# Packed attention and routed experts: the first batch's scores in two column ranges, and four of its hidden blocks as split products

## The chip, the cores and the metric

One core of a Trainium2 chip. The metric is the device time of one execution, in microseconds (us); the time of a kernel is the median of its runs. Engines by their names in the profile: PE (matmuls) with PEld (its weight loads), DVE (VectorE), ACT (ScalarE), POOL (GpSimd), SP (SyncE, which here issues most DMAs).

## The reference, cut to what matters

```python
def sm_attn(qq, kk, vv):                       # scale = 1/8
    s = scale * qq @ kk.T;  s -= s.max(-1)
    a = exp(s);  a /= a.sum(-1) + 1e-9
    return a @ vv
p_packed = sm_attn(p, k, v)                    # 32 packed rows for each of 8 batches x 8 heads
x = sm_attn(q, p_packed, p_packed)             # 576 rows of 64 for each head -> (4608, 512)
logits = (x / |x|) @ (emb / |emb|).T / tau     # 8 experts
e = argmax(logits);  gate = softmax(logits)[e]
out = gate * (relu(x @ w1[e]) @ w2[e])         # 512 -> 1024 -> 512, fp32
```

## The kernel before

The eight batches are worked one after the other, each with its own 576 rows, eight heads in two groups of four (g = 0, 1; heads of a group lie side by side in 128 partitions). For each batch the kernel packs (32 packed rows for each head), guesses from the sum of the packed rows which expert the whole batch takes, loads that expert's w1 and w2 only, and later counts the rows that took another expert, which a loop at the end would redo. Every tile's engine is chosen by hand; each engine, and each DMA queue, runs its instructions in the order in which the program emits them.

Because a batch's x is its softmax times the packed rows, the first expert layer is done as softmax times G, where G is packed rows times w1 (128 rows for a group, 1024 columns in two halves fc = 0, 1). A product in full fp32 (two MATMUL records each) is used in a few places; most are "split": both factors are kept as a high and a low part (a cast, then a subtraction), and three products high x high, high x low, low x high are summed, each one MATMUL record (type fp32r).

The first batch goes ahead of the steady state, and the change is all in it:

- `begin` (lines 1024 to 1181) is emitted in pieces, each letter q of `PLAN` being one. Its first piece issues the loads of k, v and q (`load_whole`, `load_v`: lines 190, 201), turns the keys block by block on DVE (`flip`, lines 285 to 287), scores them on PE (`quarters`, line 238), takes maximum and exponential (350, 355), turns the result on PE (370), multiplies by v (390), sums the packed rows (402, 1096, 1101), and makes the guess (533 to 551; SP reads the index at line 551). `load_w1` (764) follows on SP, then k tiles of the second batch (175). After the guess come the transposes of q (1136) and its scores (1146). The fourth to sixth q pieces split the packed rows and their logits into `ppx` (274, 275), a factor of the routing products.
- `embeddings` (124) normalises the expert rows with a chain of small POOL steps (98 to 139), stepped by `next(emb_gen)`.
- The softmax of the first batch's 576 rows in two halves (hf = 0, 1) follows `ORDS`, one step for each letter s: U turn back, B biggest, S subtract, X exponential, T total, N normalise, R turn, H high part (619), L low part (623). `ENG` says for S, N and L, and for the four splits of G, whether POOL (p) or DVE (v) does them.
- `ffn` with late=True is the first batch's expert stage. It multiplies packed rows by w1 (853, `rows_w1`, g = 0 then 1), copies the result (863), and runs 16 hidden blocks: eight of half 0 (f0 to f7) and eight of half 1 (here h0 to h7). Before the change all of f0 to f7 are two full fp32 products each (872, one for each g; those of g = 0 of f0 to f3 early), and h0 to h7 are six split products each (893), which need all of G and of the high and low parts. Each block goes to one of four PSUM banks (tag pf), and the block four later waits until ACT's relu (897) and DVE's low part (898, and 903 in half 1) have read it. Then come eight steps over f at line 924 (the rest rows), interleaved with routing, and the output products (940).
- After each block the loop runs one string of `PLAN`: q a piece of `begin`, s a softmax step, G one split of G (`split_g`, 274 and 275), a a step of the second batch's attention (`att_main(1)`: scale and turn p, lines 301 and 302; four key flips; key scores, 260; maximum and exponential of each group, 350 and 355; turn of group 0, then of group 1 with its copies, 370 and 381 to 384; values, 390), w a split of w2 (`split_w2`, 785 on ACT and 786 on POOL), k a query flip (290, 294), r a step of routing (`route`, 680 on PE, 689 on DVE, 696 on ACT, five chunks through two PSUM tiles of tag pb).

## Time and profile before

| | us |
|---|---|
| runs of the kernel before | 444.05, 445.36, 445.59 (median 445.36) |
| the profiled execution: its own time | 444.3 |
| its span, first to last instruction | 442.6 |
| PE busy | 430.8 (97% of the span) |
| DVE, ACT, POOL busy | 303.3, 203.6, 150.2 |
| bytes moved by DMA | 88.22 MB, 199 GB/s in the mean |

The span is 1.7 us under the execution's own time, and the rows below are all of this one execution. A timeline row merges instructions of one line: start, time from the first start to the last end, engine, line, operation, tiles, shape, count, and in brackets the idle time before it with what ended it. PE's ends are modelled, so a stretch without an idle gap can still hold waits; the distance from one start to the next tells more.

### The profile page before, as it was taken

What the parts mean: (1) busy time and instruction counts of PE and PEld (TensorE: products, weight loads), DVE (VectorE), ACT (ScalarE), POOL (GpSimd) and SP (SyncE); (2) the same over time, 40 slices, a digit from 0 to 9 for tenths busy, and PEclk for the clock granted to TensorE, in tenths of its full rate; (3) what the DMA queues carried; (4) which work ended last, traced back from release to release, by engine and by line L of the source; (5) the groups of instructions that cost most, each with busy time, mean ns of one, the idle gap of its engine ahead of it and who ended that gap; (6) DMA issues with size and microseconds to landing.
All of it is one profiled execution on the core that took longest, in us unless ns stands there. A gap on an engine that the chain in (4) does not pass through costs nothing.

```text
span 442.6 us, 10441 instructions
## 1 busy us (share of the span) xinstructions
PE 430.8 (97%) x3762; PEld 339.4 (77%) x3763; DVE 303.3 (69%) x1006; ACT 203.6 (46%) x477; POOL 150.2 (34%) x201
## 2 busy tenths in 40 slices
PE   8799999999999999999999999999999999999994
PEld 6537768798787978879687977879687886879784
DVE  5568759669965899469883799558994698535400
ACT  2457632773237723465127723366235751466110
POOL 2538645342404441152504523044501534035000
PEclk9999999999999999999999999999999999999998
DMA  7999988877985479944995389843998206500011
GB/s 208 290 282 286 232 213 325 246 180 204 321 301 141 110 216 360 275 113 138 298 364 143 88 231 353 268 128 102 241 386 243 79 1 220 221 26 24 15 48 54
DMA packets 40267, 88.22 MB, mean 199 GB/s; under 512 B 10312, under 2 KB 19848, under 8 KB 40208
## 3 DMA queue, kind: packets, MB, share of 16 engines
q1 hardware_dynamic: 31920, 57.96, 46.2%
q0 software_dynamic: 8000, 29.43, 18.3%
q8 instruction: 32, 0.52, 0.5%
q14 instruction: 27, 0.22, 0.2%
q10 hardware_dynamic: 288, 0.08, 0.1%
HBM read 78.00 MB, written 9.44 MB: 198 GB/s over the span
## 4 chain that ended last, share of the span: by engine, by line
PE 89%; DMA 6%; DVE 2%; ACT 1%; SPq 1%; issue 0%; DVEq 0%; ACTq 0%
PE pf L940 41%; PE pf L893 21%; PE pf L924 6%; PE pt L680 6%; PE pt L260 4%; PE pt L810 3%; PE pt L390 3%; DMA nat<-in_v 2%; DMA nat<-in_q 2%; PE pt L370 1%; DMA w1t<-in_moe_w 1%; PE pf L853 1%; DVE hT L898 1%; PE pt L853 1%; PE pf L872 0%; SPq L201 0%
## 5 line engine op out<-in xcount | busy, mean ns | idle before, releaser
L940 PE MATMUL pf<-w2s,hT 128*128 128x512 f32 (+1 forms) x792 | 189.1, 390 | 0.0
L940 PEld LDWEIGHTS pf<-w2s,hT 128*128 128x128 f32 x792 | 142.1, 188 | 37.4 <-issue 6.7
L786 POOL TENSOR_TENSOR w2s<-w2r,w2s 128x512 fp32r<-128x512 f32 x64 | 82.6, 1292 | 178.3 <-ACT w2s L785 176.6
L893 PE MATMUL pf<-AT,G 128*128 128x288 f32 x720 | 105.0, 299 | 0.1
L893 PEld LDWEIGHTS pf<-AT,G 128*128 128x128 f32 x720 | 97.5, 188 | 5.1 <-issue 2.3
L897 ACT ACTIVATE hT<-pf 128x224 fp32r<-128x224 f32 (+1 forms) x128 | 48.1, 388 | 43.7 <-PE pf L893 42.4
L898 DVE SCALAR_TENSOR_TENSOR hT<-pf,hT 128x224 fp32r<-128x224 f32 (+1 forms) x128 | 52.4, 414 | 16.3 <-ACT hT L897 16.3
L696 ACT ACTIVATE at<-pt 128x512 f32<-128x512 f32 (+1 forms) x40 | 23.9, 598 | 40.9 <-DVE lg L689 40.2
L785 ACT CAST w2s<-w2r 128x512 fp32r<-128x512 f32 x64 | 39.8, 623 | 1.2 <-issue 1.2
L1200 ACT ACTIVATE o<-pf,gate 128x512 f32<-128x512 f32 (+1 forms) x41 | 26.0, 634 | 29.2 <-PE pf L940 18.6
L680 PEld LDWEIGHTS pt<-ppx,AT 128*128 128x128 f32 (+1 forms) x240 | 33.2, 177 | 6.0 <-ACT at L696 1.4
L680 PE MATMUL pt<-ppx,AT 128*128 128x264 f32 (+1 forms) x240 | 36.4, 287 | 0.5
L924 PE MATMUL pf<-w2r,h 128*64 128x256 f32 x256 | 34.1, 390 | 0.0
L689 DVE TENSOR_REDUCE lg<-pt 128x8 f32<-128x16 f32 (+1 forms) x40 | 6.9, 171 | 36.4 <-PE pt L680 36.4
L290 DVE STREAM_TRANSPOSE kt<-nat 128x512 f32<-128x512 f32 x28 | 31.2, 1120 | 0.0
L824 DVE TENSOR_TENSOR G<-pt,G 128x512 fp32r<-128x512 f32 x28 | 18.8, 688 | 14.4 <-ACT G L823 14.4
L592 ACT ACTIVATE st<-st 128x576 f32<-128x576 f32 (+1 forms) x17 | 11.2, 658 | 30.1 <-DVE st L589 29.4
L275 POOL TENSOR_TENSOR ppx<-pp,ppx 128x256 fp32r<-128x256 f32 x16 | 11.5, 739 | 38.7 <-ACT ppx L274 38.7
L924 PEld LDWEIGHTS pf<-w2r,h 128*64 128x64 f32 x256 | 15.7, 136 | 9.8 <-issue 4.3
L619 ACT CAST AT<-at 128x576 fp32r<-128x576 f32 x16 | 10.8, 673 | 20.3 <-DVE at L613 20.3
L775 POOL DMA_DIRECT2D w2r<-in_moe_w x28 | 19.7, 712 | 0.0
L823 ACT CAST G<-pt 128x512 fp32r<-128x512 f32 x28 | 15.8, 588 | 7.1 <-DVE G L824 4.5
(181 smaller groups left out, 479.9 us busy)
## 6 DMA issues: line engine op xcount, KB each, us to landing
nat<-in_k SPq DMA_DIRECT2D x112, 140.0 KB, 3.4
nat<-in_q SPq DMA_DIRECT2D x112, 140.0 KB, 4.0
w1t<-in_moe_w POOLq DMA_DIRECT2D x14, 1024.0 KB, 8.3
w2r<-in_moe_w POOLq DMA_DIRECT2D x28, 512.0 KB, 11.1
out<-o SPq DMA_DIRECT2D x27, 256.0 KB, 3.3
nat<-in_v SPq DMA_DIRECT2D x32, 160.0 KB, 4.1
nat<-in_v SPq DMA_DIRECT2D x32, 128.0 KB, 4.1
w1t<-in_moe_w SPq DMA_DIRECT2D x4, 512.0 KB, 6.1
```

Source lines behind the costliest of these rows:

```text
L290: nc.vector.transpose(kt[:, :512].rearrange("p (c i a) -> p c a i", a=4, i=32), t[:, :16].rearrange("p (c a) d -> p c a d", a=4),)
L680: nc.tensor.matmul(pt[:r, 512 * g : 512 * g + XW], AT[:, a, g, c * P : c * P + r], x.ppx[:, m, g], start=(i == 0), stop=(i == 2),)
L696: nc.scalar.activation(scr[:r, :, : HB * D], ptv[:r, :, 0 : HB * D], AF.Square, accum_out=ss[:r, c : c + 1])
L775: queue.dma_start(t, w2e[:, 2 * i : 2 * i + 2, :])
L785: nc.scalar.copy(t[:, 0], raw)
L786: nc.gpsimd.tensor_tensor(out=t[:, 1], in0=raw, in1=t[:, 0].bitcast(F32), op=ALU.subtract)
L893: nc.tensor.matmul(pf[:, :HS], w, r, start=(n == 0), stop=(n == len(ops) - 1))
L897: nc.scalar.activation(hT[:, 0, f, cs], pf[:, :n], AF.Relu)
L898: nc.vector.scalar_tensor_tensor(out=hT[:, 1, f, cs], in0=pf[:, :n], scalar=0.0, in1=hT[:, 0, f, cs].bitcast(F32), op0=ALU.max, op1=ALU.su ...
L924: nc.tensor.matmul(pf[64 * hf : 64 * hf + 64, :256], h4[:, f], x.w2r[f // 2][:, f % 2, hf * 256 : hf * 256 + 256], start=(f == 0), stop=(f ...
L940: nc.tensor.matmul(pf[:, :w], hT[:, a, f, c * P : (c + 1) * P], x.w2s[f][:, m, at : at + w], start=(f == 0 and i == 0), stop=(f == NF - 1 ...
L1200: nc.scalar.activation(o[:, :w], pf[:, :w], AF.Copy, scale=x.gate[:, c : c + 1])
```

## The change

- `begin`: tau is loaded from ACT's queue in place of POOL's, and the embedding rows are scaled on POOL in place of ACT. The keys of both groups are scored in the column ranges 0 to 255 and 256 to 575 (`CUT`); group 1 is also flipped range by range (`flip_part`: ten turns in place of six), with a maximum and an exponential for each range. The three embedding steps stand together after group 0. Dummy products `warm(4)` and `warm(1)` stand ahead of the turns of the two groups; the turned halves are copied in smaller pieces, group 0 by DVE, group 1 by ACT. The packed rows' copy `rows2`, its turn into `Tw` and the products `pp4` move ahead of the guess. The q transposes go eight to a PSUM tile, those of group 1 after the first scores.
- `ORDS`: high and low part of half 0 move from the end to behind the turn of half 1's predecessor (H0 after R0b, L0 after T1). `ENG`: both low parts go from POOL to DVE.
- `split_g` takes the four parts in the order (fc 1, g 0), (0, 0), (1, 1), (0, 1), and two of them are emitted before the last w1 products' copies. f4 to f7 become six split products each.
- `PLAN`: key scores are emitted after h5 (before: after h1), and with them the maxima, exponentials and turns move later; the splits of w2 stand differently (seven ahead of the last `ppx` piece, five before); routing begins at the sixth of the eight steps of line 924 (before: the fourth).

```diff
-        nc.scalar.mul(en_sb, emb_sb, enrm)
+        nc.gpsimd.tensor_scalar(out=en_sb, in0=emb_sb, scalar1=enrm, scalar2=None, op0=ALU.mult)
...
+    def flip_part(t, ko, e, n0, n1, tail):
...
+        nc.vector.transpose(k4[:, :2, n0:n1], ti[:, :, n0:n1])
+        nc.vector.transpose(k4[:, 2:, n0:n1], tj[:, :, n0:n1])
+        if tail:
+            nc.vector.transpose(ko[:, 512:].rearrange("p (a i) -> p a i", i=32), ti[:, :, 4])
...
+    GORD = ((1, 0), (0, 0), (1, 1), (0, 1))
...
-        fc, g = x.gs // NG, x.gs % NG
+        fc, g = GORD[x.gs]
...
-            assert not late or hf == 0 or x.soft and x.gs >= NG * (f // 4 + 1)
-            if late and hf == 0:
-                for g in range(f in opened, NG):
-                    first_half(f, g)
+            assert not late or hf == 0 and (f < HB or x.gs > 2) or x.soft and x.gs == 4
+            if f in opened and hf == 0:
+                first_half(f, 1)
                 pf = opened[f]
...
-        nc.gpsimd.dma_start(itau, tau.broadcast_to([P, 1]))
+        nc.scalar.dma_start(itau, tau.broadcast_to([P, 1]))
...
+        CUT = (slice(0, 256), slice(256, S))
...
+            kts = [sb.tile([P, S], F32, name="kt", tag="kq", bufs=8) for _ in range(2)]
+            for n, cols in enumerate(CUT):
+                for e in range(2):
+                    flip_part(kn[g], kts[e], e, 2 * n, 2 * n + 2, n)
+                    quarters(into, pw[:, 1, g, e], kts[e], lambda c: head(g, c), cols, e)
...
+        warm(WARM[1])
+        turned = turn_bank()
+        turn_keys(0, enumerate(blocks(turned, NC5)))
...
+        warm(WARM[2])
+        turn_keys(1, zip((0, 1), blocks(halves[0], 2)))
+        nc.scalar.copy(flat[1][:, :256], halves[0][:, :256])
+        turn_keys(1, zip((2, 3, 4), blocks(halves[1], 3)))
+        nc.scalar.copy(flat[1][:, 256:], halves[1][:, :256])
...
-    WARM = (13, 0)
+    WARM = (13, 4, 1)
...
-    ORDS = "U0a B0a S0a X0a U0b B0b T0a S0b X0b T0b N0a N0b R0a U1 B1 S1 X1 R0b T1 N1 R1 H1 L1 H0 L0"
-    ENG = "pvpppppppp"
+    ORDS = "U0a B0a S0a X0a U0b B0b T0a S0b X0b T0b N0a N0b R0a U1 B1 S1 X1 R0b H0 T1 L0 N1 R1 H1 L1"
+    ENG = "pvppvvpppp"
...
-        "qssq", "sssssssss", "sss", "ss", "ss", "ssG", "", "sG", "ssa", "ssa",
-        "a", "sa", "a", "GG", "w", "aa", "aq", "w", "aw", "aq",
-        "aw", "aw", "aq", "k", "q", "rwrkw", "k", "rk", "rrr", "arrrrw",
+        "qssq", "sssssssss", "sss", "ssG", "ssGsss", "sG", "", "", "s", "G",
+        "ss", "a", "sa", "a", "aw", "a", "w", "", "w", "aa",
+        "aqw", "aaw", "aq", "aqw", "aw", "qw", "rk", "rkrk", "rkrr", "arrrr",
```

The first string runs before the expert stage. The next five stand behind its five yields up to the second copies; then eight behind f0 to f7, eight behind h0 to h7 (the 14th string, counted from 0, is the one behind h0), and eight behind the steps of line 924.

## Rows read from the trace of the kernel before

**Rows 1.** The page's busy times, and busy time of each engine in four stretches (stretch, its length, then busy us and instructions of PE, PEld, DVE, ACT, POOL, then the granted clock, the DMA engines' share, GB/s).

```profile
PE 430.8 (97%) x3762; PEld 339.4 (77%) x3763; DVE 303.3 (69%) x1006; ACT 203.6 (46%) x477; POOL 150.2 (34%) x201
...
31.00:46.00 15.00, 14.63 (x106) 11.12 (x105) 11.90 (x37) 11.07 (x28) 12.55 (x12) 1.00 0.89 271
46.00:59.00 13.00, 12.57 (x166) 8.34 (x164) 8.78 (x31) 8.59 (x23) 6.93 (x9) 1.00 0.92 227
59.00:431.00 372.00, 371.97 (x3161) 298.84 (x3160) 264.71 (x846) 170.59 (x398) 119.38 (x149) 1.00 0.63 195
```

**Rows 2.** The chain of work that ended last, its first 60 us (start, length, what).

```profile
2.29 6.99 DMA nat<-in_v
9.29 9.14 DMA nat<-in_q
18.45 4.54 DMA w1t<-in_moe_w
```

**Rows 3.** SP's queue in the first 30 us: what its issues waited for (us in total, times, longest), then the read of the guessed index and the w1 load from the views of their lines (the last row is of the w1 load).

```profile
SPq L201 <- DMA pn<-in_p: 1.0, 1, 1.0
...
SPq L764 <- DMA nat<-in_q: 0.2, 1, 0.2
...
L551 SPq TENSOR_LOAD <-idx x1: 464/464/464, 17.3 to 17.3; - x1
...
DMA to landing us min/median/max: 4.5/6.1/9.0
```

**Rows 4.** Timelines of the front: PE's key scores, turn and values of group 1, the sum, the guess; a DVE flip of group 1, its maximum; ACT's first work after its two DMA issues; the issues of p on POOL.

```profile
7.62 3.17 PE L238 MATMUL pt<-kt,pw 32*32 32x288 f32 x48
12.54 0.77 PE L370 MATMUL pt<-ident,p 128*128 128x128 f32 x5 [0.60 <-ACT p L355]
14.28 0.90 PE L390 MATMUL pf<-nat,p1T 128*32 128x64 f32 x40
16.47 0.34 PE L533 MATMUL pu<-enT,total 128*1 128x8 f32 x8 [0.41 <-DVE total L1101]
...
7.83 0.45 DVE L285 STREAM_TRANSPOSE kt<-nat 128x256 f32<-128x256 f32 x1 [0.33 <-DMA nat<-in_k]
10.86 0.76 DVE L350 TENSOR_REDUCE mx<-pt 128x1 f32<-128x576 f32 x1 [0.67 <-PE pt L238]
...
2.03 1.28 ACT L130 ACT_TABLE_LOAD   x1 [1.90 <-issue]
5.55 0.63 ACT L130 ACTIVATE esq<-emb_sb 8x512 f32<-8x512 f32 x1 [2.24 <-DMA emb_sb<-in_moe_expert_emb]
...
13.42 2.26 POOL L213 DMA_DIRECT2D pn<-in_p  x4
```

**Rows 5.** PE's timeline from the w1 products to the first output products.

```profile
30.95 4.34 PE L872 MATMUL pf<-at,g 128*128 128x288 f32 x16
35.58 2.38 PE L872 MATMUL pf<-at,g 128*128 128x288 f32 x8 [0.29 <-DVE hT L898]
...
40.00 1.20 PE L260 MATMUL pt<-kt,pw 64*32 64x288 f32 x32
41.13 5.07 PE L893 MATMUL pf<-AT,G 128*128 128x288 f32 x36
...
49.82 2.09 PE L680 MATMUL pt<-ppx,AT 128*128 128x264 f32 x12
...
59.03 1.66 PE L940 MATMUL pf<-w2s,hT 128*128 128x512 f32 x6
```

**Rows 6.** DVE's timeline around the flips (start, length; the next row's start tells how long DVE was held).

```profile
32.89 0.77 DVE L613 STREAM_TRANSPOSE at<-st 128x576 f32<-128x576 f32 x1
33.58 0.42 DVE L898 SCALAR_TENSOR_TENSOR hT<-pf,hT 128x288 fp32r<-128x288 f32 x1
33.92 0.92 DVE L301 TENSOR_SCALAR pbd<-pn 128x128 f32<-128x128 f32 x1
34.87 0.31 DVE L302 STREAM_TRANSPOSE pw<-pbd 128x128 f32<-128x128 f32 x1
35.11 0.42 DVE L898 SCALAR_TENSOR_TENSOR hT<-pf,hT 128x288 fp32r<-128x288 f32 x1
35.45 0.43 DVE L285 STREAM_TRANSPOSE kt<-nat 128x256 f32<-128x256 f32 x1
...
36.25 0.42 DVE L898 SCALAR_TENSOR_TENSOR hT<-pf,hT 128x288 fp32r<-128x288 f32 x1
```

**Rows 7.** DVE instructions that read one or two SBUF tiles, over the whole span, with and without a POOL instruction beside them (duration ns least/median/longest).

```profile
L589 DVE TENSOR_TENSOR st<-st,mx x15: 694/758/1057, 27.1 to 375.3; 128x576 f32<-128x576 f32 x15
...
L301 DVE TENSOR_SCALAR pbd<-pn x7: 217/221/918, 33.9 to 330.9; 128x128 f32<-128x128 f32 x7
```

**Rows 8.** ACT's and POOL's timelines: the second exponential of the second batch's keys, the two copies; POOL's splits and the logits' low part.

```profile
46.13 0.74 ACT L355 ACTIVATE p<-pt,mx 128x576 f32<-128x576 f32 x1 [0.70 <-DVE mx L350]
...
48.38 1.08 ACT L381 COPY p1T<-pt 128x512 f32<-128x512 f32 x2
...
47.55 2.52 POOL L786 TENSOR_TENSOR w2s<-w2r,w2s 128x512 fp32r<-128x512 f32 x2 [0.87 <-ACT w2s L785]
50.01 0.23 POOL L275 TENSOR_TENSOR ppx<-m,ppx 128x16 fp32r<-128x16 f32 x1
```

**Rows 9.** What PE's routing products (line 680) waited for, 46 to 60 us (us in total, times).

```profile
  POOL ppx L275: 0.3, 1
```

More of the change, by code (lines that the diff above doesn't have):

```diff
@@ L1059, in begin, with scored @@
         )
+        CUT = (slice(0, 256), slice(256, S))
+        def scored(g, cols=slice(0, S)):
+            return x.s1[g][:, 256 + cols.start : 256 + cols.stop]
         for g in range(NG):
             x.s1[g] = turn_bank()
-            for e in range(2):
-                kt = flip(kn[g], True, e)
-                for hf in range(2):
-                    quarters(x.s1[g], pw[:, 1, g, e], kt, lambda c: head(g, c), hf, hf, e)
-            next(emb_gen)
-            if g == 0:
-                next(emb_gen)
@@ L1069, in begin @@
-        prefetch(1)
-        key_max(x, 0)
-        key_exp(x, 0)
-        key_max(x, 1)
-        pt = turn_bank()
-        p1_turn(x, 0, pt, pt[:, 512:])
-        key_exp(x, 1)
-        p1_evac(x, 0, pt, pt[:, 512:], 0)
-        nc.vector.reciprocal(itau, itau)
+            into = scored(g)
+            if g == 0:
+                for e in range(2):
+                    kt = flip(kn[g], True, e)
+                    for cols in CUT:
+                        quarters(into, pw[:, 1, g, e], kt, lambda c: head(g, c), cols, e)
+                for _ in range(3):
+                    next(emb_gen)
+                continue
@@ new lines, in begin, with turn_keys @@
+        for n, cols in enumerate(CUT):
+            nc.scalar.activation(
+                x.p1[1][:, cols], scored(1, cols), AF.Exp, bias=x.mx[1],
+                **(dict(accum_out=x.sums[1]) if n else {}),
+            )
+        flat = []
+        for g in range(NG):
+            tag = ("p1T", "w2s")[g]
+            x.p1T[g] = sb.tile([P, NC5, P], F32, name="p1T", tag=tag, bufs=(2, NF)[g])
+            flat.append(x.p1T[g][:, 0:4].rearrange("p a b -> p (a b)"))
+        def turn_keys(g, places):
+            for c, at in places:
+                r = rows(c)
+                nc.tensor.transpose(at[:r], x.p1[g][:, c * P : c * P + r], ident)
@@ new lines, in blocks @@
+        def blocks(pt, n):
+            return [pt[:, i * P : i * P + P] for i in range(n)]
+        warm(WARM[1])
+        turned = turn_bank()
+        turn_keys(0, enumerate(blocks(turned, NC5)))
+        for cols in (slice(0, 256), slice(256, 512)):
+            nc.vector.tensor_copy(flat[0][:, cols], turned[:, cols])
+        nc.vector.tensor_copy(x.p1T[0][:64, 4], turned[:64, 512 : 512 + P])
+        key_sum(x, 0)
+        nc.vector.reciprocal(itau, itau)
+        halves = [bank() for _ in range(2)]
@@ L1083, in begin @@
+        nc.vector.tensor_reduce(part, x.p1[1][:, CUT[0]], axis=AX.X, op=ALU.add)
+        nc.vector.tensor_tensor(out=x.sums[1], in0=x.sums[1], in1=part, op=ALU.add)
         key_sum(x, 1)
-        po = [bank()]
+        next(emb_gen)
+        spare = sb.tile([P, NG * (2 * D + NCB * D)], F32, name="spare", tag="hT")
+        rows2 = spare[:, : NG * 2 * D].rearrange("p (g t d) -> p g t d", g=NG, t=2)
         pack_tiles(x)
-        pack_values(x, 0, vn[0], po[0])
-        p1_evac(x, 1, pt, pt[:, 512:], 512, "w2s")
@@ L1088, in begin @@
-        pair_rows(x, 0, po[0])
-        next(emb_gen)
-        po.append(bank())
-        pack_values(x, 1, vn[1], po[1])
+        po = [bank() for _ in range(NG)]
+        for g in range(NG):
+            pack_values(x, g, vn[g], po[g])
+            pair_rows(x, g, po[g])
+            nc.scalar.mul(rows2[:, g], po[g][:, :D].unsqueeze(1).broadcast_to([P, 2, D]), x.rinv[g])
         drain(emb_gen)
-        pair_rows(x, 1, po[1])
         pt = ps.tile([P, 512], F32, name="pu", tag="pf")
```

81 lines of the change are left out of this document (48 added, 33 removed).

## The prediction

> **What bounds the kernel now.** I read the busy times and the stretches first [rows 1]. From 59 to 431 us PE is busy 371.97 of 372.00 us: whatever time the first batch gains or loses before 59 us goes to the end unchanged, and nothing behind it changes. The change touches only what stands before, so the question is when the first output product (line 940) starts, 59.03 us now [rows 5].
>
> Before that there are two regimes. Up to 23 us the chain of waits is almost all transfers: in_v until 9.28, in_q until 18.43, w1 until 22.99 [rows 2]. From 31 to 59 us PE is busy 27.2 of 28 us [rows 1], but its ends are modelled, and its row has gaps closed by DVE's hT [rows 5]: there PE and DVE bind in turn.
>
> **The front: no gain.** The scores in ranges do shorten the compute chain. Group 1's six turns take 1.6 us from 7.83; ten smaller ones, at 0.19 to 0.24 each for a 128x128 block (the higher figure is p's turn, from its start to the next row's [rows 6]), take 1.8 to 2.1, but PE can start after the first two of them, and its scores should end about 10.4 in place of 10.8 [rows 4]. The maximum of the first range overlaps the rest, and the exponential is done some 0.2 us sooner. Three things stop this gain.
>
> 1. Group 1's products with v start at 14.28 [rows 4]. They need the last of v. Each DMA issue that waits, waits for the landing of the one eight issues earlier in program order: SP's fifth v load for p, the w1 load for in_q [rows 3]. By that count the last v load goes out when the second k lands, at 7.8, and 5.9 to 7.2 us more for it (the other v loads; I estimate from the k tiles' issues behind it that it lands at about 14.15) leave 0.1 us. From there the order is the same: sum of rows, total, guess at 16.47. The two turns of `rows2` (0.44 us) now stand between sum and guess on PE, but fall in the 0.41 us in which PE waits for `total` [rows 4]. I take 0.0, with -0.1 to +0.4: four dummy products of 0.2 to 0.4 us each could hold the turn of group 0 back by up to 0.7, of which some 0.3 are covered.
> 2. SP reads the index at 17.3 (0.46 us) and is ready near 18.25; it then waits 0.2 us for the second q load [rows 3]. Seven k loads still stand between the two, so the eight-back count still holds the w1 load to q's landing at 18.43 [rows 2]. A guess that is earlier gains nothing; one later by over 0.2 us costs.
> 3. The four w1 loads land 4.5 to 9.0 us after their issue [rows 3], the last at 20.1 + 9.0 = 29.1, about when PE comes to it. The DMA engines are the limit here.
>
> The rest of the front I cost at nothing, with its cover: tau's DMA on ACT goes out while ACT waits until 5.55 for the embeddings [rows 4]; the embedding rows on POOL stand behind p's four issues (2.26 us), but the small-step chain starts 2 us sooner, since its second DVE step now stands before group 1's flips instead of behind them, so they should be scaled by about 14.5, and PE wants them at 15.1. `rows2` and `Tw` on ACT and `pp4` on POOL only swap places with work that PE had not reached. Without these covers each is worth 0.3 to 0.7 us. The q transposes end within 0.2 us of before and w1 lands later. Sum of the front: 0.0, range -0.2 to +0.5.
>
> **f4 to f7.** Two full products take 1.05 to 1.1 us for a block (24 records of line 872 from 30.95 to 37.96: 12 products in 7.0 us with 0.5 of waits), six split ones 0.82 (36 records, six blocks, 5.07) [rows 5]. Four blocks: 1.0 us of PE less. The low parts of half 0 and of G's fc = 1 must be there: the casts and subtractions fall in ACT's and POOL's time before 32, and G's last piece comes some 0.35 us late for f4. PE would finish h7 near 45.0 instead of 46.0, if DVE let it.
>
> **DVE in the same stretch.** Its order, with the time from each start to the next [rows 6]: hT of half 0 0.34, R1 0.69, a key flip 0.80 (three turns, 35.45 to 36.25), hT and its rest in half 1 0.43, p's scaling 0.22 and turn 0.24. The low parts come from POOL: 0.7 to 0.76 each as the 128x576 subtraction beside it [rows 7]. L0 falls into DVE's idle time before 32.5. From 32.5: hT f0, f1, R1, f2, f3 (2.05) to 34.6; L1, behind its cast and POOL's last G split, to 35.8; hT f4, p (0.8) to 36.6; then three times hT and a flip (3.4) to 40.0; h0, the fourth flip, h1 (1.65) to 41.7. PE needs h1's bank for h5, so h5 runs 41.8 to 42.6, and key scores, now behind h5, start at 42.6 instead of 40.0 [rows 5].
>
> Here a row speaks against the change: the same DVE subtraction took 1.057 us where a POOL subtraction lay beside it and 0.694 at best, and p's scaling 0.918 in this very stretch against 0.22 [rows 7]. I charge L1 0.4 us for it (POOL's split is nearly through when L1 is ready); p's scaling is now free of POOL and gives back 0.7. The Trainium skill (SBUF — State Buffer, "Who interferes with whom") says that the instruction that issues first keeps the shared port pair for its whole length and the other fully blocks. By it L1 could lose a whole POOL instruction, 1.25 us, and the forecast would be about 0.9 us later.
>
> **What the later key scores delay.** This is where the gain goes. From key scores at 42.6: scores ready 43.95; first maximum 0.75; but ACT takes h6's relu first, and the exponential runs 45.05 to 45.75; its sum and the second maximum on DVE to 47.1; second exponential (0.71 of ACT) 47.15 to 47.9. Before, it started at 46.13 [rows 8]. The turn of group 1 waits for it: PE stands some 0.5 us before 48.15. Then ACT works through two small casts (0.45), a w2 cast (0.5), the two copies (1.0), another w2 cast (0.5), and only then, at 50.35, the logits' high part. POOL has two w2 splits of 1.26 before the logits' low part [rows 8]: the second starts at 50.5, so the low part is there at 52.0; before, at 50.24. Routing's first products need it: line 680 already waited 0.3 us for just this [rows 9]. PE, which has done five of the eight steps of line 924 by 49.75, finds nothing else in its order and idles about 2.2 us, until 52.0 instead of starting at 49.82 [rows 5].
>
> From there PE has five routing chunks (0.75 each), three steps (0.47), the values (1.66) and the counts (0.25): 7.1 us, and waits of some 0.5 for the two routing tiles, which DVE and ACT empty between query flips. Line 940 then starts at 52.0 + 7.6 = 59.6 or 59.7. Against 59.03: **+0.6 to +0.7 us**.
>
> **Sum.** Front 0.0, stage +0.7. The profiled execution took 444.3 us (span 442.6), so 445.0 for one like it; the median of the runs is 1.06 above that, so on the median 445.36 + 0.7 = **446.0**. This kernel's runs differ by 1.5 us; about 0.5% (2.2 us) is what a measurement of it can tell from no change, so I forecast no change that can be told, with a small loss in it.
>
> **Rivals.**
>
> 1. The products' saving stays. If the low part of the logits is there before PE wants it (the exponentials half a microsecond sooner each, or POOL free), PE loses only the 0.5 before the turn of group 1, and gains 1.0 on f4 to f7 and up to 0.8 on old waits. Line 940 at 57.9 to 58.5: -0.6 to -1.1, 444.2 to 444.8; I put it at 444.5. For it: PE has 97% [rows 1], and DVE and ACT have 3 us of slack in 31 to 46. Against it: all six steps from key scores to routing hang on one another, and seven w2 splits now stand ahead of the last piece instead of five.
> 2. The front pays: if transfers shift so that the second q load lands sooner, w1 comes sooner by as much; half a microsecond, with the stage's loss 445.5; with the stage's saving about 443.9, and beyond 2.2 us only if both are at their best.
> 3. Slower, by one mechanism: ACT held by tau's DMA. SP's fifth v load waited 1.0 us for p and held all behind it [rows 3]. If tau's DMA counts among the first eight it waits for nothing; if it counts behind the v and q loads, it waits on ACT's queue for a v load near 10.0, and the table load (1.28) and the square of the embeddings (0.8) come behind it [rows 4]. DVE's first embedding step then stands ahead of group 1's flips and waits too: flips at 12.6 instead of 7.8. Of the 4.8 us some 0.5 are covered; w1 goes out 4.2 us late, into nearly empty DMA engines, which give back about a microsecond: +3.3, 449.4 with the stage's loss. The point from which it decides: ACT's square starting after 7 us. Program order puts the DMA third on ACT, at about 2.0 us, when fewer than eight are out, which speaks against it. The Trainium skill (DMA: Bandwidth & Descriptors, "Anatomy of one DMA") states that a DMA's wait for a semaphore is spent on the issuing sequencer before dispatch: it is ACT that would stand.
>
> **How the numbers follow.** Forecast (445.2 to 447.4: POOL's port up to +0.9, front up to +0.5): 0.54. Rival 1: 0.27. Rival 2: 0.10. Rival 3: 0.09. The range takes in rival 1 with its lower bounds and the forecast with its upper ones, 444.0 to 447.8, and leaves out rival 3 and the best of rival 2. Faster by over 0.5% (under 443.1) needs rivals 1 and 2 together: 0.06; slower (over 447.6): rival 3 and a little of the forecast's own tail: 0.12; within: 0.82.
>
> **What would show it.** In the profile after: w1's first product within 0.3 us of 23.13; f4 to f7 as sets of six at 0.82; key scores between 42.2 and 43; PE idle 1.5 to 2.5 us before the first product of line 680, released by POOL's ppx; that product near 52. Wrong if line 680 starts before 50.5, if key scores come before 41.5, or if the guess's product moves by over 0.5 us from 16.47.

## The result, and the profile after

The changed kernel took 448.01 us (median of 4 runs, 447.51 to 448.18), the kernel before 444.71 us on the same chip (4 runs, 443.91 to 445.59): a ratio of 1.0073, 95% interval 1.0056 to 1.0089. It is 3.3 us slower, more than the half per cent that can be told from no change, and above the forecast range of 444.0 to 447.8. The profiled execution took 447.51 us, with a span of 445.9.

PE's timeline of the changed kernel, from the embeddings' transposes to the second group of split rows (start, length, engine, line, what, instructions, and in brackets the idle time ahead and what ended it; line 544 is the guess's product, 1194 the q transposes, 1214 the first scores, 865 the w1 products):

```profile
15.52 0.41 PE L148 MATMUL pf<-ident,en_sb 8*128 8x8 f32 x4 [0.95 <-POOL en_sb L144]
...
16.87 0.34 PE L544 MATMUL pu<-enT,total 128*1 128x8 f32 x8
17.15 1.09 PE L1194 MATMUL pt<-ident,nat 128*128 128x128 f32 x8
18.08 0.27 PE L1194 MATMUL pf<-ident,nat 128*128 128x128 f32 x1
19.73 1.37 PE L1214 MATMUL pt<-spare,tw 64*32 64x288 f32 x16 [1.38 <-DVE spare L1200]
21.04 1.97 PE L1194 MATMUL pt<-ident,nat 128*128 128x128 f32 x8
22.80 0.42 PE L1194 MATMUL pf<-ident,nat 128*128 128x128 f32 x1
24.33 1.22 PE L1214 MATMUL pt<-spare,tw 64*32 64x288 f32 x16 [1.12 <-ACT spare L1201]
...
26.10 3.55 PE L865 MATMUL pf<-w1t,tw 64*32 64x512 f32 x16
30.35 2.21 PE L884 MATMUL pf<-at,g 128*128 128x288 f32 x8 [0.71 <-ACT g L875]
32.49 1.92 PE L865 MATMUL pt<-w1t,tw 64*32 64x512 f32 x16
34.34 2.21 PE L884 MATMUL pf<-at,g 128*128 128x288 f32 x8
```

The guess comes within the range that I gave it, at 16.87 for 16.47 [rows 4], though TensorE stood for 0.95 us ahead of the embeddings' transposes. Then it stands for 1.38 us and for 1.12 us, the second group's q transposes end at 23.2 and the first w1 product comes at 26.10. Two more views of the changed kernel tell why the first gap is there: ACT's timeline, and in the second block DVE's.

```profile
18.28 0.59 ACT L1200 COPY spare<-pt 128x512 f32<-128x512 f32 x1 [1.12 <-PE pt L1194]
18.76 0.27 ACT L1201 COPY spare<-pf 128x128 f32<-128x128 f32 x1
```

```profile
18.89 0.69 DVE L1200 COPY spare<-pt 128x512 f32<-128x512 f32 x1 [0.78 <-ACT spare L1200]
```

All eight transposes now write one two-bank tile. ACT's copy of its first half starts behind the last of them, and DVE's copy of the other half behind ACT's, not beside it. In the kernel before, with a tile for each copy, DVE's ran beside ACT's and waited for PE alone:

```profile
17.66 0.81 ACT L1139 COPY spare<-pf 128x512 f32<-128x512 f32 x2
18.09 0.69 DVE L1139 COPY spare<-pf 128x512 f32<-128x512 f32 x1 [0.39 <-PE pf L1136]
```

In the changed kernel the second group's transposes stand behind the first group's scores and so behind both copies. The stretches of the changed kernel show what else happens there (stretch, length, busy time and instructions of PE, PEld, DVE, ACT, POOL, granted TensorE clock, DMA share, GB/s):

```profile
17.00:19.00 2.00, 1.35 (x17) 1.07 (x14) 0.86 (x6) 0.88 (x3) 0.00 (x0) 1.00 0.87 217
19.00:21.00 2.00, 1.27 (x16) 0.40 (x16) 0.59 (x1) 0.03 (x1) 0.00 (x0) 0.54 0.67 238
21.00:29.00 8.00, 6.88 (x50) 2.93 (x43) 3.77 (x11) 2.40 (x6) 2.01 (x3) 0.50 1.00 299
...
56.00:60.00 4.00, 4.00 (x21) 3.20 (x21) 2.77 (x7) 1.38 (x4) 0.74 (x3) 0.59 0.54 142
```

The granted clock is 0.50 (the lower level, 1.2 GHz) for some 10 us from 19.2, so the first sixteen w1 products take 3.55 us where the next sixteen, at 1.00, take 1.92. It falls again from 56.7 to 60.1. In the profile of before it is 1.00 in both places ([rows 1] and this stretch):

```profile
17.00:31.00 14.00, 12.09 (x95) 5.28 (x93) 9.05 (x25) 6.12 (x13) 3.90 (x6) 1.00 0.94 278
```

Around that second fall PE's timeline of the changed kernel reads:

```profile
46.24 1.20 PE L260 MATMUL pt<-kt,pw 64*32 64x288 f32 x32
...
53.99 0.39 PE L691 MATMUL pt<-ppx,AT 128*128 128x264 f32 x1 [0.53 <-ACT ppx L274]
55.42 0.88 PE L691 MATMUL pt<-ppx,AT 128*128 128x264 f32 x5 [1.03 <-POOL ppx L275]
...
56.85 3.01 PE L691 MATMUL pt<-ppx,AT 128*128 128x264 f32 x12
...
60.52 1.72 PE L691 MATMUL pt<-ppx,AT 128*128 128x264 f32 x12
...
64.69 1.65 PE L951 MATMUL pf<-w2s,hT 128*128 128x512 f32 x6
```

The first output product comes 5.66 us later than in [rows 5], yet the span grew by 3.3 only: 2.4 us come back behind it, where I had said that nothing changes. The group row of the output products shows the place (line, what, instructions, then busy us and mean ns of one, idle). Kernel before:

```profile
L940 PE MATMUL pf<-w2s,hT 128*128 128x512 f32 (+1 forms) x792 | 189.1, 390 | 0.0
```

Changed kernel:

```profile
L951 PE MATMUL pf<-w2s,hT 128*128 128x512 f32 (+1 forms) x792 | 186.4, 387 | 0.0
```

The same 792 products are busy 2.7 us less. From one start to the next (mean of the distances between 200 and 300 ns) they stand 232.5 ns apart before and 228.5 ns after.

So three things had to be explained: the query section, the stage, and faster output products that no line of the change speaks of. One candidate for the last: the tile `spare`, of tag hT, is now taken ahead of the packed tiles. Tiles of one tag share a place, and the hidden rows hT use this one later; so hT now lies at byte 113760 of a partition, in place of 134368.

### The profile page after: what moved, and what is told of

It is laid out like the page before. It is cut to its first block, busy times and chain, and to the rows that moved or that the text cites. A ratio compares the mean times of both kernels' runs of the same rounds, so it can differ in the third digit from the quotient of the medians.

```text
span 445.9 us, 10490 instructions
## 1 busy us (share of the span) xinstructions
PE 431.9 (97%) x3780; PEld 342.7 (77%) x3781; DVE 306.7 (69%) x1017; ACT 203.8 (46%) x478; POOL 148.7 (33%) x199
## 4 chain that ended last, share of the span: by engine, by line
PE 87%; DVE 4%; DMA 3%; ACT 2%; POOL 2%; issue 1%; SPq 0%; DVEq 0%; ACTq 0%; POOLq 0%
PE pf L951 37%; PE pf L904 21%; PE pt L691 7%; PE pf L935 7%; PE pt L260 4%; PE pt L822 3%; PE pt L401 3%; DMA nat<-in_q 2%; PE pt L381 1%; DMA pn<-in_p 1%; PE pf L865 1%; PE pt L1194 1%; PE pt L1214 1%; POOL pn L213 1%; PE pf L884 0%
## 5 line engine op out<-in xcount | busy, mean ns | idle before, releaser
L951 PE MATMUL pf<-w2s,hT 128*128 128x512 f32 (+1 forms) x792 | 186.4, 387 | 0.0
L904 PE MATMUL pf<-AT,G 128*128 128x288 f32 x744 | 108.9, 299 | 0.5 <-DVE h L914 0.4
L904 PEld LDWEIGHTS pf<-AT,G 128*128 128x128 f32 x744 | 100.9, 188 | 6.2 <-issue 2.8
L691 PEld LDWEIGHTS pt<-ppx,AT 128*128 128x128 f32 (+1 forms) x240 | 34.5, 185 | 7.0 <-POOL ppx L275 1.2
L691 PE MATMUL pt<-ppx,AT 128*128 128x264 f32 (+1 forms) x240 | 37.5, 294 | 1.8 <-POOL ppx L275 1.0
L836 DVE TENSOR_TENSOR G<-pt,G 128x512 fp32r<-128x512 f32 x28 | 18.8, 688 | 14.5 <-ACT G L835 14.5
```

Of the source, the lines that this page charges most:

```text
L691: nc.tensor.matmul(pt[:r, 512 * g : 512 * g + XW], AT[:, a, g, c * P : c * P + r], x.ppx[:, m, g], start=(i == 0), stop=(i == 2),)
L904: nc.tensor.matmul(pf[:, :HS], w, r, start=(n == 0), stop=(n == len(ops) - 1))
L951: nc.tensor.matmul(pf[:, :w], hT[:, a, f, c * P : (c + 1) * P], x.w2s[f][:, m, at : at + w], start=(f == 0 and i == 0), stop=(f == NF - 1 ...
```

## Experiments

Times are medians, each with the ratio to the kernel before in the same batch of runs.

**e1, the query section of before**, with a PSUM bank of its own for every call of `turn_queries`. In the changed kernel, cut to the order of the calls:

```
-        turn_queries(0, (nc.scalar.copy, nc.vector.tensor_copy))
-        first_scores(0)
-        turn_queries(1, (nc.scalar.copy, nc.scalar.copy))
+        turn_queries(0, 0, 4, nc.scalar.copy)
+        turn_queries(0, 4, 4, nc.vector.tensor_copy)
+        turn_queries(0, 8, 1, nc.scalar.copy)
+        turn_queries(1, 0, 4, nc.scalar.copy)
+        first_scores(0)
+        turn_queries(1, 4, 4, nc.scalar.copy)
+        turn_queries(1, 8, 1, nc.scalar.copy)
```

> The changed kernel with one part taken back: the query section between the guess and the first w1 products is that of before (the q transposes of each group in banks of four, four and one, with a copy behind each bank, the second group's first four ahead of the first group's scores, the PSUM tiles of the scores taken at the start). Theory A (the +3.3 us of the result are lost in the query section, where the copies of one two-bank tile go one behind the other and the TensorE clock then falls to 0.50 from 19.6 to 29.2 us): first w1 product at 23.1 to 23.6 instead of 26.10, granted clock 1.00 from 17 to 31 us, time 444.3 to 445.3. Rival B (the clock falls for another reason, such as the dummy products that now run earlier): the granted clock still is 0.50 for some 10 us after 19 us, and the time stays at 446.5 or more.

Measured 445.65 us, ratio 1.0036 (1.0022 to 1.0051): +1.6 us for +3.3, so 1.7 us of the loss are gone. Stretches of this kernel, columns as above:

```profile
17.00:20.00 3.00, 3.00 (x22) 2.77 (x21) 1.28 (x6) 1.23 (x3) 0.11 (x1) 0.51 0.54 144
20.00:24.00 4.00, 3.24 (x46) 1.38 (x46) 1.78 (x5) 1.75 (x5) 0.67 (x1) 1.00 0.95 330
```

The clock fell here too, even earlier, so half of theory A is wrong: the query section doesn't cause the fall. But TensorE had its transposes to do without a gap, the clock was back after some 3 us, and from the guess's product to the first w1 product it took 6.29 us:

```profile
17.19 0.34 PE L544 MATMUL pu<-enT,total 128*1 128x8 f32 x8
23.48 2.65 PE L865 MATMUL pf<-w1t,tw 64*32 64x512 f32 x16
```

Rival B's lasting fall didn't come either. What the time has above theory A's 445.3 isn't taken apart; the execution profiled, of 445.20 us, has the second fall too, from 54.1 to 57.5.

**e2, six dummy products in the gap.** In the changed kernel:

```
+        pd = bank()
+        for _ in range(6):
+            nc.tensor.matmul(pd[:, :P], ident, ident, start=True, stop=True)
         first_scores(0)
```

> The changed kernel with six more 128x128 dummy products (identity by identity, their result is read by nobody) between the first group's q transposes and its scores, where TensorE stood for 1.38 us. The order of the query section stays that of the change. Theory A1 (most of the loss is the clock that falls after the gap): the granted clock stays at 1.00 from 19 to 31 us and the first w1 product comes at 23.8 to 24.6 instead of 26.10, time 445.4 to 446.6. Theory A2 (most of the loss is the order, copies in series and the second group's transposes behind the scores; the clock only goes with it): w1 products at 25.5 or later though the clock is at 1.00, time 447.2 or more.

Measured 445.88 us, 1.0049 (1.0031 to 1.0067), 1.4 us of the loss gone. The clock didn't stay at 1.00, it fell at 17.1, but it was back at 20.5, while the dummies ran. The first w1 product came at 25.59, where A2 had it, and the time is where A1 had it; neither is right as stated. Part of the gain is that this profile has no second fall.

```profile
17.43 0.35 PE L544 MATMUL pu<-enT,total 128*1 128x8 f32 x8
...
21.50 0.71 PE L1214 MATMUL pt<-spare,tw 64*32 64x288 f32 x16
...
25.59 1.93 PE L865 MATMUL pf<-w1t,tw 64*32 64x512 f32 x16
```

From the first scores on this profile has the new order at 1.00: 4.09 us to the first w1 product, where it took 6.37 in the changed kernel (19.73 to 26.10).

**e3, hT moved and nothing else.** In the kernel before:

```
+        spare = sb.tile([P, NG * (2 * D + NCB * D)], F32, name="spare", tag="hT")
         pack_tiles(x)
...
-        spare = sb.tile([P, NG * (2 * D + NCB * D)], F32, name="spare", tag="hT")
```

> The kernel before with one line moved: the spare tile of tag hT is taken ahead of the packed tiles, so that the hidden rows hT lie at byte 113760 of a partition, as in the changed kernel, instead of 134368. No instruction is added, removed or moved. Theory P (the 2.4 us that the changed kernel gets back between the first output product and the end come from where hT lies): the output products' spacing falls from a mean of 232.5 ns to 228.5 ns, and the time from 444.7 to 442.0 to 442.8. Rival Q (they come from the split order, the order of the w2 tiles or another thing in the changed kernel): spacing 232.5 ns, time 444.4 to 445.0.

Measured 441.58 us, 0.9947 (0.9934 to 0.9959). The output products of this kernel:

```profile
L940 PE MATMUL pf<-w2s,hT 128*128 128x512 f32 (+1 forms) x792 | 186.4, 387 | 0.0
```

Spacing 228.4 ns. Theory P holds, on the kernel before, with not one instruction changed.

**e4, hT moved back.** In the changed kernel, the packed tiles and the w1 tile are taken ahead of `spare`:

```
-        w1t = sb.tile([P, NPR, F], F32, name="w1t", tag="w1t")
+        w1t = x.w1t if whole else sb.tile([P, NPR, F], F32, name="w1t", tag="w1t")
...
+        pack_tiles(x)
+        x.w1t = sb.tile([P, NPR, F], F32, name="w1t", tag="w1t")
         spare = sb.tile([P, NG * (2 * D + NCB * D)], F32, name="spare", tag="hT")
...
-        pack_tiles(x)
```

> The changed kernel with hT back at byte 134368 of a partition (its tile is taken behind the packed tiles and the w1 tile, as before); nothing else is changed. Theory P (the place of hT sets the spacing of the output products): spacing 232.5 ns instead of 228.5 ns, time 450.0 to 450.9. Rival Q: spacing 228.5 ns, time 447.7 to 448.4.

Measured 449.80 us, 1.0126 (1.0111 to 1.0141), 5.8 us over before: this is what the change costs without what hT's place gives. Its output products:

```profile
L951 PE MATMUL pf<-w2s,hT 128*128 128x512 f32 (+1 forms) x792 | 189.0, 390 | 0.0
```

**e5, the stage alone.** The kernel before with the change's `hidden`, `GORD`, `ORDS`, `ENG` and `PLAN`, of which two are shown:

```
-    ORDS = "U0a B0a S0a X0a U0b B0b T0a S0b X0b T0b N0a N0b R0a U1 B1 S1 X1 R0b T1 N1 R1 H1 L1 H0 L0"
+    ORDS = "U0a B0a S0a X0a U0b B0b T0a S0b X0b T0b N0a N0b R0a U1 B1 S1 X1 R0b H0 T1 L0 N1 R1 H1 L1"
-    ENG = "pvpppppppp"
+    ENG = "pvppvvpppp"
```

> The kernel before with only the second half of the change: f4 to f7 as six split products each, the new order of the splits of the w1 rows, two of them on VectorE, the key scores' logits later, and the new plan of the w2 splits. The front and the query section stay as before, hT stays at byte 134368. Forecast of the prediction: +0.7 us, 444.7. Theory C (the routing products also wait for the packed logits' low part on GpSimd, TensorE stands for 0.5 and 1.0 us ahead of them as in the changed kernel, and in some executions the clock falls after that): first output product 1.5 to 2.5 us later than the 59.03 us of before, time 445.2 to 446.6. Rival D (without the late w1 products of the changed front the stage gains): time 443.0 to 444.0.

Measured 446.06 us, 1.0042 (1.0028 to 1.0056): +1.6 us, as theory C had it. PE's timeline of this kernel:

```profile
34.65 6.41 PE L893 MATMUL pf<-AT,G 128*128 128x288 f32 x43 [0.63 <-POOL G L275]
...
43.47 1.20 PE L260 MATMUL pt<-kt,pw 64*32 64x288 f32 x32
...
51.22 0.39 PE L680 MATMUL pt<-ppx,AT 128*128 128x264 f32 x1 [0.52 <-ACT ppx L274]
52.65 0.88 PE L680 MATMUL pt<-ppx,AT 128*128 128x264 f32 x5 [1.04 <-POOL ppx L275]
...
60.67 1.66 PE L940 MATMUL pf<-w2s,hT 128*128 128x512 f32 x6
```

The two waits are those of the changed kernel, without its second fall, and the first output product is 1.64 us later than in [rows 5].

**e6, the w2 splits later.** In the changed kernel's plan of the stage ("q" at this place is the split of the packed logits, "w" a w2 split):

```
-        "aqw", "aaw", "aq", "aqw", "aw", "qw", "rk", "rkrk", "rkrr", "arrrr",
+        "aqw", "aaw", "aq", "aq", "a", "qwww", "rk", "rkrk", "rkrr", "arrrr",
```

> The changed kernel with two of the w2 splits (the copy on ScalarE and the low part of 1.28 us on GpSimd) moved behind the split of the packed logits, where one stood already. Theory C (the routing products stand for 0.53 and 1.03 us because GpSimd does two low parts of w2 ahead of the low part of the logits, and the clock falls after that from 56.9 to 60.1 us): the second routing product follows the first within 0.4 us, granted clock 1.00 from 50 to 65 us, time 445.0 to 446.6 (the front's loss stays). Rival E (what TensorE waits for there is the key scores that come later, not GpSimd's queue): the same wait with another name, time 447.4 or more.

Measured 445.15 us, 1.0018 (1.0009 to 1.0028): +0.7 us for +3.3. PE's timeline of this kernel:

```profile
54.61 1.01 PE L691 MATMUL pt<-ppx,AT 128*128 128x264 f32 x6
...
56.14 1.73 PE L691 MATMUL pt<-ppx,AT 128*128 128x264 f32 x12
```

Both waits are gone and so is the second fall, though the first one lasted 13.6 us here (16.9 to 30.5). What TensorE waited for was GpSimd's queue, not the key scores: rival E falls.

**e7, the embeddings on ScalarE again.** In the changed kernel:

```
-        nc.gpsimd.tensor_scalar(out=en_sb, in0=emb_sb, scalar1=enrm, scalar2=None, op0=ALU.mult)
+        nc.scalar.mul(en_sb, emb_sb, enrm)
```

> The changed kernel with the scaling of the expert embeddings on ScalarE again instead of GpSimd, where it took 1.57 us and TensorE stood for 0.95 us before the embeddings' transposes. Theory F (that idle time is what the first fall of the granted clock follows, in all four runs of the changed front so far): the embeddings' transposes come within 0.3 us of the last value product, the granted clock is 1.00 from 15 to 31 us, and the time is 444.8 to 446.2. Rival G (the clock falls for the gap of 1.38 us before the first scores, or for the weak activity before it): the granted clock still falls to 0.50 between 17 and 20 us, time 446.8 or more.

Measured 445.46 us, 1.0018 (1.0005 to 1.0032): +1.0 us for +3.3. The scaling takes 0.72 us instead of 1.57 and the idle 0.95 us are gone. The clock stays at 1.00 until 20, but then it falls, behind the gap of 1.38 us, and is back at 23.4:

```profile
16.18 0.34 PE L544 MATMUL pu<-enT,total 128*1 128x8 f32 x8
...
19.04 1.92 PE L1214 MATMUL pt<-spare,tw 64*32 64x288 f32 x16 [1.38 <-DVE spare L1200]
...
25.21 1.93 PE L865 MATMUL pf<-w1t,tw 64*32 64x512 f32 x16
```

```profile
17.00:20.00 3.00, 1.48 (x16) 0.73 (x20) 1.05 (x3) 0.75 (x2) 0.00 (x0) 1.00 0.89 222
20.00:24.00 4.00, 3.07 (x23) 1.78 (x9) 0.94 (x2) 1.10 (x3) 0.67 (x1) 0.58 0.97 358
```

F's time with G's clock: taking one gap away moved the fall, it didn't remove it. This profile has no second fall.

**e8, hT moved, the stage, and the splits later**, on the kernel before (e3, e5 and e6's edits).

> The kernel before with hT at byte 113760, with the stage part of the change, and with the w2 splits behind the packed logits as in the run with the later splits; the front stays as before. If the three effects add up (the place of hT -2.4 us, f4 to f7 -1.0 us, no wait for GpSimd): 440.2 to 441.4, faster than both kernels and than before with hT moved alone (441.6). If the later key scores cost what the split products save: 441.4 to 442.2.

Measured 441.76 us, 0.9939 (0.9927 to 0.9951), no better than e3, in the range that was expected if the later key scores cost what f4 to f7 save; which part of the stage takes the saving back wasn't told apart further. First output product at 58.79, at 58.68 in e3.

**e9, the front alone.** The changed kernel with `hidden`, `GORD`, `ORDS`, `ENG` and `PLAN` of before.

> The changed kernel with the stage of before (f4 to f7 as whole and half products, the order and plan of the splits, the early key scores), so that only the front, the query section and the place of hT are changed. Theory H (the front and query section cost 3 to 4 us, the place of hT gives 2.5 us back, the second fall of the clock belongs to the stage): time 444.6 to 446.0, one fall of the granted clock, between 16 and 30 us, none from 50 to 65 us, output products at 228.4 ns. Rival I (front and stage only hurt together): 442.0 to 443.2.

Measured 445.32 us, 1.0029 (1.0020 to 1.0039). Against e3, which has hT at the same place, the ratios give +0.8%, 3.6 us: theory H. One fall of the clock, 17.2 to 24.0, none later; the products of line 951 at 228.5 ns.

**e10, three repairs at once**: the edits of e1, e6 and e7 in the changed kernel.

> The changed kernel with three repairs at once: the query section of before, the embeddings' scaling on ScalarE, and the two w2 splits behind the packed logits. What stays of the change: the guess's second group in two ranges with dummies, f4 to f7 as split products with the later key scores, hT at byte 113760. If these three places are the whole of the loss: 441.4 to 442.4, as before with hT moved (441.6), and no fall of the granted clock after 31 us. If something else in the changed front costs time: 443.0 or more.

Measured 442.10 us, 0.9954 (0.9936 to 0.9971): -2.2 us for +3.3, so 5.5 us better than the changed kernel. PE's timeline of this kernel:

```profile
16.13 0.34 PE L544 MATMUL pu<-enT,total 128*1 128x8 f32 x8
...
22.95 2.37 PE L865 MATMUL pf<-w1t,tw 64*32 64x512 f32 x16
...
50.44 1.01 PE L691 MATMUL pt<-ppx,AT 128*128 128x264 f32 x6
...
58.62 1.65 PE L951 MATMUL pf<-w2s,hT 128*128 128x512 f32 x6
```

No fall of the clock in this profile. These three places are the whole of the loss; the guess in two ranges and the rest of the stage, which stay in, give and cost nothing that shows (-2.4 us in e3, which is without them).

**e11 to e18, where hT lies.** All are the kernel before with tiles taken in another order or with unused bytes between them, and no other instruction. e11 takes `spare` between the packed tiles and the w1 tile, e12 between the w1 tile and the packed tiles. e13 to e17 are e3 with free bytes ahead of and behind hT, 256 together, so that all tiles above lie alike; e14 for one:

```
+        sb.tile([P, 32], F32, name="pada", tag="pada")
         spare = sb.tile([P, NG * (2 * D + NCB * D)], F32, name="spare", tag="hT")
+        sb.tile([P, 32], F32, name="padb", tag="padb")
```

e18 has 32 free bytes ahead of the w2 tiles and 224 ahead of hT.

> The kernel before with hT at byte 117984: the packed tiles stay at 113760, the w1 tile goes to 150752 as in the changed kernel. Same instructions. If the spacing of the output products hangs on where the w1 tile lies (150752: fast) or on hT lying mostly below some byte between 113760 and 134368: about 228.4 ns and 441.2 to 442.4. If it hangs on hT at 113760 exactly, or on the packed tiles: 232.5 ns and 444.0 to 445.0.

> The kernel before with the w1 tile at byte 113760, hT at 130144 and the packed tiles at 162912. Same instructions. If what counts is hT's first half (the high parts, which two of three output products take as weights) lying low, it now starts 4224 bytes ahead of before's place and 16384 above the fast one: spacing near before's 232.5 ns and 444.0 to 445.0. If any order with hT ahead of the packed tiles is fast: 228.4 ns and 441.2 to 442.4.

> Before with hT at byte 113760 and 256 bytes left free behind it: control for the three runs that follow. All tiles above hT move up by 256 bytes. If hT's own place decides: spacing 228.4 ns, 441.2 to 442.4. If what counts is hT against a tile above it: spacing changes.

> The same with 128 free bytes ahead of hT and 128 behind: hT at 113888, whose remainder by 256 is 224, as at the two slow places. If that remainder of hT's own place decides: spacing 232.5 ns, 444.0 to 445.0. If the order of the tiles decides: 228.4 ns, 441.2 to 442.4.

> The same with 32 free bytes ahead of hT and 224 behind: hT at 113792, remainder 128 by 256. No earlier run has this remainder: fast (228.4 ns or less, 440.5 to 442.4) or slow (232.5 ns, 444.0 to 445.0) places it.

> The same with 160 free bytes ahead of hT and 96 behind: hT at 113920, remainder 0 by 256. If even starts matter, the spacing goes below 228.4 ns and the time below 441.2; if only a few remainders are slow, 228.4 ns and 441.2 to 442.4.

> As the control with the free bytes behind hT, but all 256 ahead of it: hT at byte 114016, remainder 96 by 256 but 352 by 512; all tiles above as in the control, the w2 tiles from 17504 as before. If the fast place repeats every 256 bytes: spacing 228.4 ns, 441.2 to 442.4. If it takes 512 or more: 232.5 to 233.4 ns, 444.0 to 445.0.

> hT at byte 114016 as in the run before this one, and the w2 tiles and all that lies between moved up by 32 bytes, so that w2 starts at remainder 128 by 256 and hT at 96. If hT's own byte decides: the same spacing as with hT at 114016 and w2 unmoved. If it is hT against the w2 tiles (both at remainder 96): 232.5 to 233.4 ns and 444.0 to 445.0 where the unmoved one has 228.4 ns.

| run | hT at byte | hT, w2 (remainder by 256) | busy us of the output products | spacing ns | us | ratio (95%) |
|---|---|---|---|---|---|---|
| e11 | 117984 | 224, 96 | 189.2 | 232.6 | 444.60 | 1.0008 (0.9996 to 1.0021) |
| e12 | 130144 | 96, 96 | 186.4 | 228.5 | 441.61 | 0.9948 (0.9933 to 0.9963) |
| e13 | 113760 | 96, 96 | 186.4 | 228.5 | 441.64 | 0.9932 (0.9908 to 0.9956) |
| e14 | 113888 | 224, 96 | 189.1 | 232.5 | 444.49 | 1.0001 (0.9989 to 1.0014) |
| e15 | 113792 | 128, 96 | 189.6 | 233.4 | 444.65 | 1.0006 (0.9992 to 1.0020) |
| e16 | 113920 | 0, 96 | 189.8 | 233.3 | 444.85 | 1.0011 (0.9997 to 1.0024) |
| e17 | 114016 | 96, 96 | 186.4 | 228.5 | 441.97 | 0.9942 (0.9922 to 0.9963) |
| e18 | 114016 | 96, 128 | 189.4 | 233.0 | 444.39 | 1.0000 (0.9990 to 1.0009) |

e12 gave the second of its two expectations, and so led to the rest: hT high up is fast as well, so it isn't low addresses. With hT ahead of the packed tiles 128 or 32 bytes more make it slow (e14, e15), so it isn't the order either, and 256 more make it fast again (e17). And with hT left at its fast place and the w2 tiles moved by 32 bytes it is slow (e18): hT's own byte doesn't decide alone. The output products read hT as weights and w2 as the moving operand. They are fast in the layouts where both start at remainder 96 by 256, and slow in all in which one of the two starts elsewhere. No run has both at another equal remainder, so that it is the difference that counts, and not 96 itself for each, is likely but not shown. The tiles between w2 and hT moved with w2 in e18; they are no operands of these products.

e16 gave one thing more. Its front is that of before, and the clock fell there too:

```profile
17.00:20.00 3.00, 3.00 (x22) 2.66 (x28) 1.00 (x3) 1.35 (x4) 0.00 (x0) 0.53 1.00 253
```

Its first w1 product stands at 22.97 all the same (23.13 before), and its first output product at 58.65 (59.03 in [rows 5]).

## Why the prediction was wrong, step by step

In the sum there were two terms, front 0.0 and stage +0.7. Measured: front +3.6 (e9 against e3), stage +1.6 (e5; 1.9 by its ratio), and a third term that the sum didn't have, hT's place, -2.4 (e3). By the ratios that is +0.82, +0.42 and -0.53%, together +0.71 of the measured +0.73%: nothing is left over that these runs can tell. Where the second fall of the clock comes it costs 1.3 us (3.01 us for twelve products of line 691 in place of 1.73); the profile of the stage alone doesn't have it, and how much of the medians it makes stays open.

**The step that failed** is the last sentence but one of the front: "The q transposes end within 0.2 us of before and w1 lands later." They ended at 23.2 instead of 20.5, and w1's first load, landing 3.4 us after its issue at 18.7, was there at 22.1. I had costed two edits at nothing, one tile of two banks with two copies, and the second group's transposes behind the first group's scores, and named w1's landing as their cover, with every row read at a clock of 1.00. From the guess's product to the first w1 product it takes 6.66 us before and 9.23 in the changed kernel. Where the embeddings are on ScalarE, so that nothing else differs in the front, it is 9.03 with the new query section (e7: 25.21 less 16.18) and 6.82 with the old one (e10: 22.95 less 16.13). These 2.2 us aren't the order alone, since e7 ran at half rate from 20.0 to 23.4 and e10 never did. At full clock I estimate the new order at 2.86 us from the guess's product to the first scores (in e7 and in the changed kernel, in which the half rate begins behind the products of this stretch) and 4.09 from there to w1 (e2), together 6.95: 0.1 to 0.3 us more than the old one. The other 2.1 to 2.3 us come with the half rate, and they count because the order has used up the cover. With the old order a fall that lasts as long leaves 6.29 us (e1) or 6.82 to 6.87 (e5, e16, e18). The runs of e7 bear this out: the three with a mean granted clock of 0.998 or 0.999 took 444.15, 444.19 and 445.18 us, the nine below it 445.15 to 447.53.

The loss of the cover was readable: the diff puts all eight transposes into one tile, and a copy on ACT, 0.59 us, and one on DVE, 0.69 us, each lie on the path if they can't overlap. Whether the chip or the program's own order of accesses to one tile puts them in series, no run tells.

A second cover failed with it. The embeddings on GpSimd, which I wanted done at 14.5, were done at 15.47: 1.57 us where ACT took 0.72. TensorE idled 0.95 us for them, and the guess's product came at 16.87, where it comes at 16.18 and 16.13 with the scaling on ScalarE (e7, e10). So this edit, costed at nothing, cost 0.7 us of TensorE's path; of the 2.3 us that go with it in e7 the rest goes with the clock, which in that profile is at half rate for 3.4 us in all, in that of the changed kernel for 13.6.

**What the clock adds.** I took rows at 1.00 for granted. The fall itself isn't the change's: of the twelve profiles with before's front (before, e3, e5, e8, e11 to e18) e5, e16 and e18 have it as well, for 3 to 4 us around 17 to 21. There it costs 0.2 us or so: 6.82 to 6.87 us from the guess's product to w1's first, for 5.96 to 6.71 in the nine without it, since TensorE had transposes ready and w1 was late anyway. In the changed front all six profiles with the embeddings on GpSimd have it. Three of the four of these that keep the query section as changed (the change itself, e4, e6) have it for 10 to 14 us, over two gaps of more than a microsecond and into the w1 products (3.5 us instead of 1.9). e9 got the clock back at 24, e2 with its dummies at 20.5. Why it falls in some executions of one and the same kernel stays open.

The Trainium skill (TensorE: Matmul & The Clock Gate, "Part 1: The HAM clock gate") says that the array's clock passes at half rate or in full and depends on how busy TensorE is. By that rule idle time that is called free on TensorE isn't, if the work behind it then runs at half rate. The trace agrees as far as it goes: the w1 products take 3.55 us at 0.50 and 1.92 at 1.00.

**f4 to f7, DVE's order, the later key scores.** The mechanism was right: gain on products, key scores later, then GpSimd's w2 splits ahead of the logits' low part, and TensorE idle before the routing products, released by POOL's ppx. The forecast had the low part at 52.0 and line 940 at 59.6 or 59.7; e5 has the second routing product at 52.65 and the first output product at 60.67. Four sizes were off. f4 waits 0.6 us for the low part of the last G split on GpSimd, where I had 0.35. L1, the low part on DVE, took 1.56 us in e5 (34.91 to 36.47), 0.87 over the best row [rows 7] where I had charged 0.4. Behind it two of the blocks ahead of the key scores wait 0.4 together for DVE, so key scores came at 43.47 and not at 42.6. And from the low part to line 940 it took 8.0 us for 7.6. e6 and e8 show that it was the place of two splits in GpSimd's queue: with these moved the stage costs nothing, and gains nothing.

**What was right:** tau's DMA on ACT (third, at 2.04, the square at 5.06 for 5.55 [rows 4]), so rival 3 was none; the guess's product within 0.5 us; the scores in ranges bringing no gain, so rival 2 was none either (the second q load did land sooner in this profile, at 17.67, and w1 with it, but TensorE came to w1 only at 26.10); and no saving kept, against rival 1. That GpSimd holds L1 up was right too, but not by how much: in the changed kernel it took 0.93 us, 0.24 over the best row [rows 7], in e5 and five more profiles 1.55 or 1.56. In all nine profiles with it on DVE it ended 0.6 us behind the G split on GpSimd, so it lost what was left of that instruction, up to 0.87 us, and never a whole one. Of the signs that I had named, w1's first product within 0.3 us of 23.13 is what failed first.

**The term that was missing.** That "nothing behind it changes" was argued from the instructions behind 59 us. They didn't change; the bytes that they read moved, because a tile was taken earlier in the program. That was in the diff, in the one line that takes `spare`, and no view of a profile before could have priced it.

Nothing here is clearly better than the kernel before with that line moved: 441.58 us (e3), 0.5% faster than before and 1.2% faster than the changed kernel by the two ratios.

## What to carry to other kernels

Where an edit's cost is set to nothing because a transfer covers it, work out the new end of the covered chain copy by copy, tile by tile, and put it beside the landing: a tile shared by two copies can put them in series. Then ask what the chain takes at the lower clock, for a cover that is just used up hides a fall of the clock no longer. A low-priority step in an in-order queue (here a w2 split on GpSimd, 1.28 us) can cost up to its length when the one small step that all wait for stands behind it (here two of them, 1.6 us of idle TensorE), so place the small step first. And when an allocation moves, compare the products that run longest in both builds even though no instruction of them changed.

## What was not expected of the hardware

Output products of 128x128 weights and 512 columns followed one another at 228.5 ns in the mean where both operands' tiles start at remainder 96 by 256 bytes, and at 232.5 to 233.4 ns at four other differences of the two remainders (32, 128, 160 and 224): 2.4 to 3.2 us of 441. Not all products gain: in the profile of e3 the four column blocks of a batch stand at 228.4, 226.7, 227.6 and 232.2 ns, in that of before at 232.4, 232.5, 232.7 and 232.3. The gain is in the unbroken runs. From the seventh distance of a run on, e3 has 227.1 ns and before 232.6; in groups of up to six products e3 has 233.0 and before 232.3. The fourth block is the one that the next batch's routing products cut into groups of three and six; in the seventh batch they stand in the third block, and there the third is the slow one (231.2, the fourth 228.4). Which part of the reads collides, no run here shows.

TensorE's clock fell in the front of ten of the twenty executions profiled here, with a cost between 0.2 us or so (e5, e16, e18) and the longer w1 products of the change; after the routing waits of 0.5 and 1.0 us it fell in three profiles of six (the change, e1, e4; not e2, e5, e7), and then twelve products took 2.8 to 3.0 us instead of 1.73.
